# A recurrence and a two-layer FFN on one core: every two-operand elementwise operation but the masked decays goes to VectorE

## The chip, the cores and the metric

The kernel runs on one core of one Trainium2 chip, as one launch. The core has TensorE (PE in the rows; PEld is its weight load), VectorE (DVE), ScalarE (ACT), GpSimd (POOL) and SyncE (SP), which here only issues the loads and stores. The metric is the device time of one execution in microseconds, lower is better.

## The reference

The first half is a chunked linear recurrence over 4 x 8 heads, 768 tokens, head size 32, state size 16; the second half is an FFN on the recurrence's output.

```
for c in range(nc):                       # chunks of 32 tokens
    L = np.exp(cum[:, :, :, None] - cum[:, :, None, :]) * causal
    M = np.einsum('bhin,bhjn->bhij', Cc, Bc) * L
    y_intra = np.einsum('bhij,bhjd->bhid', M, xc)
    y_inter = np.einsum('bhin,bhnd->bhid', Cc, state) * np.exp(cum)[:, :, :, None]
    y[:, :, sl] = y_intra + y_inter
    state = decay_full * state + sum_j(Bc x xc * decay_from_j)
...
x = attn_out.transpose(0, 2, 1, 3).reshape(B * S, H * D)      # 3072 x 256
h = x @ w_in                                                  # 256 x 2048
g = np.maximum(h, 0.0) + np.log1p(np.exp(-np.abs(h)))         # softplus
return (g @ w_out).astype(np.float32)                         # 2048 x 256
```

`w_in` and `w_out` arrive as 64-bit floats and are turned into 32-bit floats on the chip.

## The kernel before

**Units.** The recurrence is worked in 24 units of 128 tokens (4 batches of 6), named by a number i: `un4` is the loaded data of unit 4. For each unit the kernel makes the masked decays `rm` (`decays`, L292, on GpSimd), the scores `sp` (TensorE), their product `m` (`weigh`, L350, VectorE, reads PSUM), the scaled B `bp` (`scale_b`, L307), the scaled C in a spread layout `r_apart` (`scale_c`, L320, two halves of 64 rows), the new state (`update`, L375) from `zp` (L364), the spread state `tb` (`spread`, L383), and the output `yp` (L393 and L407). `y` (`grow`, L417) is the scaled output; ScalarE rounds it to `xh` (L419) and the low part `xl` is what is left (`rest`, L424). From unit 8 on, B and C are laid out on the chip by `split_unit` (L198 on ScalarE, L199 on VectorE: `c_all`, `b_rows`).

**FFN.** Tokens go in 6 groups j of 512 (four units), features in 16 slices k of 128. `first` (L503) makes `hp` of (j, k) from three products: high weights by `xh`, high by `xl`, low by `xh`. ScalarE applies softplus (`e`, L523) and rounds it (`gh`, L530), VectorE takes the low part `gl` (L531), and `second` (L543) adds three products into the two accumulators `acc` of group j. `hp0_14` in a row of the order is group 0, slice 14; the profile's rows leave the numbers out.

**Weights.** 16 steps, each 512 columns; even steps are `w_in`, odd ones `w_out`, and step w opens slices k = w and w + 1 (for even w). A step is: ScalarE rescales (L475), VectorE does three bit operations (L477, L479, L481), ScalarE casts the high part `wih` or `woh` (L484), and the low part `wil` or `wol` is subtracted (L486). The tile `w` has two buffers.

**Who does what.** Five kinds of work (`bp`, `r_apart`, `tb`, `xl`, `wil`/`wol`) go to VectorE for the numbers in a table and to GpSimd for the rest:

```
V_BP = (0, 2, 7)
V_CC = (0, 1, 2, 6, 7)
V_TB = (2, 3, 4, 6)
V_XL = (2, 4, 7)
WL_V = (2, 7, 10, 11, 15)
```

**Order.** Up to unit 3 an order written out by hand (`ORDER`) is kept on every engine; its instructions appear under the line of a helper, L119. From there a scheduler orders the instructions of each engine from its own estimates of their lengths. Each engine then runs its instructions strictly in that order, and one that waits holds up all behind it. SyncE's order of loads is the same before and after the change.

Of the kernel before, what the change touches and what calls it, by code (L numbers as in the profile page):

```python
# [10 lines left out]
F32 = mybir.dt.float32  # L11
# [4 lines left out]
ALU = mybir.AluOpType  # L16
PSUM = bass.MemoryType.PSUM

P = 128
# [39 lines left out]
LAG = 8  # L59
LATE = (1, 1, 1, 1, -1, -2, -1, -1)  # L60
V_LAG = (0, 0, 1, 0, 0, 2, 0, 0)

V_BP = (0, 2, 7)
V_CC = (0, 1, 2, 6, 7)
V_TB = (2, 3, 4, 6)
V_XL = (2, 4, 7)
WL_V = (2, 7, 10, 11, 15)


def constants():  # L70
# [26 lines left out]
def recurrence_then_ffn(ctx: ExitStack, tc: tile.TileContext, fst, un, at, al, w_in, w_out, const, outT):  # L97
# [24 lines left out]
    V, A, Pl, PE = (InOrder(e) for e in (nc.vector, nc.scalar, nc.gpsimd, nc.tensor))  # L122
# [153 lines left out]
    def x_parts(t0):  # L276
        j = max(i for i in range(len(sizes)) if starts[i] <= t0)
        if j not in xparts:
            xparts[j] = [p3.tile([P, 2, 512], F32R, tag=f"x{v}", name=f"x{v}_{j}", bufs=2) for v in "hl"]
        return xparts[j], t0 - starts[j]  # L280
# [4 lines left out]
    mid = defaultdict(dict)  # L285
# [17 lines left out]
    def scale_b(i):  # L303
        b, u = divmod(i, NU)
        if u < NU - 1:
            bp = mid[i]["bp"] = p2.tile([P, NH, N], F32, tag="bp", name=f"bp{i}")
            (V if i in V_BP else Pl).tensor_tensor(  # L307
                bp,
                un_s[i][:, U_B:U_C].rearrange("p (h n) -> p h n", n=N),
                f_tok[b][0][:, u, :].unsqueeze(2).broadcast_to([P, NH, N]),  # L310
                op=ALU.mult,
            )

    def scale_c(i):
        b, u = divmod(i, NU)
        if u > 0:
            cc = mid[i]["cc"] = r_apart[i % 2]
            for g in range(2):
                rows = slice(64 * g, 64 * g + 64)
                (V if i in V_CC else Pl).tensor_tensor(  # L320
                    cc[rows, g],
                    un_s[i][rows, U_C:U_S].rearrange("p (c i) -> p c i", i=SUB),
                    f_row[b][rows, u, :NC].unsqueeze(2).broadcast_to([64, NC, SUB]),
                    op=ALU.mult,
                )
# [53 lines left out]
    def spread(i):  # L379

        if i % NU > 0:
            tb = mid[i]["tb"] = p2.tile([P, 2, 2, D], F32, tag="tb", name=f"tb{i}")
            (V if i in V_TB else Pl).tensor_tensor(  # L383
                tb,
                state[i - 1].rearrange("p (e d) -> p e d", d=D).unsqueeze(1).broadcast_to([P, 2, 2, D]),
                bd.rearrange("p (q e) -> p q e", e=2).unsqueeze(3).broadcast_to([P, 2, 2, D]),
                op=ALU.mult,
            )
# [32 lines left out]
    def rest(i):  # L421
        (xh, xl), c0 = x_parts(i * P)
        hi = xh[:, :, c0 : c0 + P].bitcast(F32)
        (V if i in V_XL else Pl).tensor_tensor(xl[:, :, c0 : c0 + P], mid.pop(i)["y"], hi, op=ALU.subtract)  # L424

    def attend_scores(i):
        decays(i)
        for g in range(2):
            score(i, g)
            weigh(i, g)  # L430
        scale_b(i)
        scale_c(i)

    def attend_values(i):
        for f in (spread, update, read, within, grow, rest):
            f(i)
# [24 lines left out]
    def split_stages(step):  # L461
        raw = raws.pop(step)
        q = step // 2
        if step % 2 == 0:
            fs = slice(q * 256, q * 256 + 256)
            cut = "p (c f) -> p c f", {"c": 2}
            hi, lo = wih[:, :, fs], wil[:, :, fs]
        else:
            ks = slice(2 * q, 2 * q + 2)
            cut = "p (k e) -> p k e", {"k": 2}  # L470
            hi, lo = woh[:, ks, :], wol[:, ks, :]
        low, high = raw[:, :, 0], raw[:, :, 1]
        w = p2.tile([P, 512], I32, tag="w", name=f"w{step}")
        wf = w.bitcast(F32)
        A.activation(wf, high.bitcast(F32), AF.Copy, scale=REBIAS)  # L475
        yield
        V.tensor_scalar(w, w, 3, None, op0=ALU.logical_shift_left)  # L477
        yield
        V.scalar_tensor_tensor(w, high, SIGN, w, op0=ALU.bitwise_and, op1=ALU.bitwise_or)  # L479
        yield  # L480
        V.scalar_tensor_tensor(w, low, 29, w, op0=ALU.logical_shift_right, op1=ALU.bitwise_or)  # L481
        yield
        r = wf.rearrange(cut[0], **cut[1])
        A.copy(hi, r)  # L484
        yield
        (V if step in WL_V else Pl).tensor_tensor(lo, r, hi.bitcast(F32), op=ALU.subtract)  # L486

    def split_w(step):
        for _ in split_stages(step):
            pass  # L490
# [89 lines left out]
    def step_w(i):  # L580
        if i not in stages:
            stages[i] = split_stages(i)
        next(stages[i], None)

    def both(f, i):
# [19 lines left out]
        "W": step_w,  # L605
        "D": decays,
        "B": scale_b,
        "C": scale_c,
        "S": lambda i: both(score, i),
        "M": lambda i: both(weigh, i),  # L610
        "U": update,
        "T": spread,
        "H": first_half,
        "R": read,
        "I": within,
        "G": grow,
        "X": rest,
        "zero": lambda _: Pl.memset(c_rows.bitcast(F32), 0.0),
    }
# [92 lines left out]
```

## Time and profile before

| | |
|---|---|
| median of 3 runs | 355.83 us (354.56 to 356.6) |
| the profiled execution | 354.56 us |
| its span, first to last instruction | 352.6 us |
| TensorE busy | 332.8 us, 94% |
| VectorE busy | 196.0 us, 56% |
| ScalarE busy | 168.4 us, 48% |
| GpSimd busy | 114.0 us, 32% |
| mean granted TensorE clock | 0.98 |

The busy shares are means over stages that differ, so a stage has to be looked at by itself. TensorE's matmuls are pipelined: one of 512 columns is listed with about 0.39 us while the next begins 0.23 us later. The time outside the span is 1.96 us.

### The profile page before, as it was taken

What the parts mean: (1) busy time and instruction counts of PE and PEld (TensorE: products, weight loads), DVE (VectorE), ACT (ScalarE), POOL (GpSimd) and SP (SyncE); (2) the same over time, 40 slices, a digit from 0 to 9 for tenths busy, and PEclk for the clock granted to TensorE, in tenths of its full rate; (3) what the DMA queues carried; (4) which work ended last, traced back from release to release, by engine and by line L of the source; (5) the groups of instructions that cost most, each with busy time, mean ns of one, the idle gap of its engine ahead of it and who ended that gap; (6) DMA issues with size and microseconds to landing.
All of it is one profiled execution on the core that took longest, in us unless ns stands there. A gap on an engine that the chain in (4) does not pass through costs nothing.

```text
span 352.6 us, 5070 instructions
## 1 busy us (share of the span) xinstructions
PE 332.8 (94%) x1882; PEld 252.0 (71%) x1882; DVE 196.0 (56%) x300; ACT 168.4 (48%) x297; POOL 114.0 (32%) x142
## 2 busy tenths in 40 slices
PE   6878985999999999999999999999999999999995
PEld 3533653567677877787877787787787788888884
DVE  1676999799984545553653553754363523132231
ACT  2311835584665535454644544645353534344450
POOL 6576943557631125323143322323512000000000
PEclk9689999899999999999999999999999999999999
DMA  7889745364210752141543222552303100001001
GB/s 203 222 196 335 252 136 187 120 257 144 51 70 8 214 152 91 30 135 48 162 121 109 65 82 71 140 161 93 91 30 89 31 2 0 0 23 40 0 2 59
DMA packets 22264, 37.23 MB, mean 106 GB/s; under 512 B 1632, under 2 KB 12896, under 8 KB 22240
## 3 DMA queue, kind: packets, MB, share of 16 engines
q1 hardware_dynamic: 22240, 36.91, 34.6%
q8 instruction: 15, 0.25, 0.3%
q14 instruction: 9, 0.07, 0.1%
HBM read 29.46 MB, written 3.24 MB: 93 GB/s over the span
## 4 chain that ended last, share of the span: by engine, by line
PE 76%; DMA 9%; DVE 8%; issue 2%; SPq 2%; ACT 1%; DVEq 0%; ACTq 0%
PE acc L543 33%; PE hp L503 32%; DMA wraw<-in_w_out 3%; DMA gg<-gd 3%; PE yp L407 3%; DVE w L479 2%; PE yp L393 2%; PE sp L339 2%; SPq L128 2%; DMA head_c<-in_fst 2%; DVE gl L531 1%; DMA c_rows<-c_all 1%; DVE w L477 1%; DVE w L481 1%; PE zp L364 1%
## 5 line engine op out<-in xcount | busy, mean ns | idle before, releaser
L531 DVE TENSOR_TENSOR gl<-e,gh 128x512 fp32r<-128x512 f32 x96 | 71.5, 746 | 83.0 <-ACT gh L530 82.3
L530 ACT CAST gh<-e 128x512 fp32r<-128x512 f32 x96 | 59.3, 620 | 65.2 <-PE acc L543 64.2
L503 PE MATMUL hp<-xh,wih 128*128 128x512 f32 (+1 forms) x192 | 77.2, 405 | 6.3 <-ACT wih L484 5.1
L523 ACT ACTIVATE e<-hp 128x512 f32<-128x512 f32 x96 | 56.6, 595 | 49.6 <-DVE gl L531 42.3
L543 PE MATMUL acc<-gl,woh 128*128 128x512 f32 x192 | 75.0, 390 | 0.0
L503 PE MATMUL hp<-xl,wih 128*128 128x512 f32 (+1 forms) x192 | 74.9, 391 | 0.0
L543 PE MATMUL acc<-gh,wol 128*128 128x512 f32 x192 | 74.9, 393 | 0.0
L503 PE MATMUL hp<-xh,wil 128*128 128x512 f32 (+1 forms) x192 | 74.3, 390 | 0.0
L543 PE MATMUL acc<-gh,woh 128*128 128x512 f32 x192 | 73.1, 392 | 0.2 <-DVE o L552 0.2
L503 PEld LDWEIGHTS hp<-xh,wih 128*128 128x128 f32 x192 | 36.1, 188 | 19.4 <-ACT wih L484 6.0
L292 POOL TENSOR_SCALAR_AFFINE_SELECT rm<-fc 128x1024 f32<-128x1024 f32 x20 | 32.1, 1605 | 47.8 <-DVE m L350 47.7
L543 PEld LDWEIGHTS acc<-gh,woh 128*128 128x128 f32 x192 | 36.0, 188 | 8.2 <-issue 0.8
L503 PEld LDWEIGHTS hp<-xh,wil 128*128 128x128 f32 x192 | 36.1, 188 | 8.0 <-issue 0.2
L543 PEld LDWEIGHTS acc<-gh,wol 128*128 128x128 f32 x192 | 36.0, 188 | 7.9 <-issue 0.2
L543 PEld LDWEIGHTS acc<-gl,woh 128*128 128x128 f32 x192 | 36.1, 188 | 7.5
L503 PEld LDWEIGHTS hp<-xl,wih 128*128 128x128 f32 x192 | 36.4, 189 | 6.5 <-issue 0.2
L350 DVE TENSOR_TENSOR m<-sp,rm 128x512 f32<-128x512 f32 x40 | 26.2, 684 | 14.0 <-PE sp L339 12.5
L199 DVE SCALAR_TENSOR_TENSOR c_all<-un,kb,c_all 128x512 fp32r<-128x512 f32 x16 | 17.3, 1084 | 10.4 <-ACT c_all L198 10.2
L424 POOL TENSOR_TENSOR xl<-y,xh 128x256 fp32r<-128x256 f32 x18 | 14.0, 780 | 25.8 <-ACT xh L419 25.2
L320 POOL TENSOR_TENSOR r_apart<-un,fr 64x128 f32<-64x128 f32 x32 | 17.1, 534 | 14.1 <-DMA un<-in_un 10.1
L307 POOL TENSOR_TENSOR bp<-un,ft 128x128 f32<-128x128 f32 x15 | 7.4, 491 | 42.1 <-DMA un<-in_un 23.7
L383 POOL TENSOR_TENSOR tb<-state,kb 128x128 f32<-128x128 f32 x16 | 11.9, 744 | 23.6 <-DVE state L375 23.0
(96 smaller groups left out, 306.5 us busy)
## 6 DMA issues: line engine op xcount, KB each, us to landing
un<-in_un SPq DMA_DIRECT2D x16, 768.0 KB, 4.5
wraw<-in_w_in SPq DMA_DIRECT2D x8, 512.0 KB, 7.8
wraw<-in_w_out SPq DMA_DIRECT2D x8, 512.0 KB
c_rows<-c_all SPq DMA_DIRECT2D x32, 128.0 KB, 2.4
gg<-gd SPq DMA_DIRECT2D x16, 192.0 KB
out_t<-o SPq DMA_DIRECT2D x12, 256.0 KB
un<-in_fst SPq DMA_DIRECT2D x4, 576.0 KB, 9.6
head_c<-in_fst SPq DMA_DIRECT2D x8, 128.0 KB, 6.5
```

Of the source, the lines that this page charges most:

```text
L199: V.scalar_tensor_tensor(out, raw, g, out.bitcast(F32), op0=ALU.mult, op1=ALU.add)
L292: Pl.affine_select(out=rm.rearrange("p h c i -> p (h c) i"), in_=fc[:, u].rearrange("p h c -> p (h c)").unsqueeze(2).broadcast_to([P, NH * ...
L320: (V if i in V_CC else Pl).tensor_tensor(cc[rows, g], un_s[i][rows, U_C:U_S].rearrange("p (c i) -> p c i", i=SUB), f_row[b][rows, u, :NC]. ...
L350: V.tensor_tensor(mid[i]["m"][:, 4 * g : 4 * g + 4].rearrange("p h t -> p (h t)"), mid[i].pop(("sp", g)), mid[i]["rm"][:, 4 * g : 4 * g + ...
L383: (V if i in V_TB else Pl).tensor_tensor(tb, state[i - 1].rearrange("p (e d) -> p e d", d=D).unsqueeze(1).broadcast_to([P, 2, 2, D]), bd.r ...
L407: PE.matmul(yp[32 * hh : 32 * hh + 32, g * P : (g + 1) * P], un_s[i][:, U_X + h * D : U_X + (h + 1) * D], m[:, h, :], start=u == 0, stop=u ...
L424: (V if i in V_XL else Pl).tensor_tensor(xl[:, :, c0 : c0 + P], mid.pop(i)["y"], hi, op=ALU.subtract)
L503: PE.matmul(h[:, c0:c1], w[:, c, fs], x[:, c, c0:c1], start=i == 0, stop=i == 5)
L523: A.activation(e, h, AF.Softplus)
L530: A.copy(gh, e)
L531: V.tensor_tensor(gl, e, gh.bitcast(F32), op=ALU.subtract)
L543: PE.matmul(acc[e][:, :n], w[:, k, es], g, start=k == 0 and i == 0, stop=k == NFT - 1 and i == 2)
```

## The change

The five tables go away, and each operation that chose an engine from one is VectorE's always. Nothing else is edited.

```diff
--- before.py
+++ after.py
@@ -59,12 +59,6 @@
 LAG = 8
 LATE = (1, 1, 1, 1, -1, -2, -1, -1)
 V_LAG = (0, 0, 1, 0, 0, 2, 0, 0)
-
-V_BP = (0, 2, 7)
-V_CC = (0, 1, 2, 6, 7)
-V_TB = (2, 3, 4, 6)
-V_XL = (2, 4, 7)
-WL_V = (2, 7, 10, 11, 15)
 
 
 def constants():
@@ -304,7 +298,7 @@
         b, u = divmod(i, NU)
         if u < NU - 1:
             bp = mid[i]["bp"] = p2.tile([P, NH, N], F32, tag="bp", name=f"bp{i}")
-            (V if i in V_BP else Pl).tensor_tensor(
+            V.tensor_tensor(
                 bp,
                 un_s[i][:, U_B:U_C].rearrange("p (h n) -> p h n", n=N),
                 f_tok[b][0][:, u, :].unsqueeze(2).broadcast_to([P, NH, N]),
@@ -317,7 +311,7 @@
             cc = mid[i]["cc"] = r_apart[i % 2]
             for g in range(2):
                 rows = slice(64 * g, 64 * g + 64)
-                (V if i in V_CC else Pl).tensor_tensor(
+                V.tensor_tensor(
                     cc[rows, g],
                     un_s[i][rows, U_C:U_S].rearrange("p (c i) -> p c i", i=SUB),
                     f_row[b][rows, u, :NC].unsqueeze(2).broadcast_to([64, NC, SUB]),
@@ -380,7 +374,7 @@
 
         if i % NU > 0:
             tb = mid[i]["tb"] = p2.tile([P, 2, 2, D], F32, tag="tb", name=f"tb{i}")
-            (V if i in V_TB else Pl).tensor_tensor(
+            V.tensor_tensor(
                 tb,
                 state[i - 1].rearrange("p (e d) -> p e d", d=D).unsqueeze(1).broadcast_to([P, 2, 2, D]),
                 bd.rearrange("p (q e) -> p q e", e=2).unsqueeze(3).broadcast_to([P, 2, 2, D]),
@@ -421,7 +415,7 @@
     def rest(i):
         (xh, xl), c0 = x_parts(i * P)
         hi = xh[:, :, c0 : c0 + P].bitcast(F32)
-        (V if i in V_XL else Pl).tensor_tensor(xl[:, :, c0 : c0 + P], mid.pop(i)["y"], hi, op=ALU.subtract)
+        V.tensor_tensor(xl[:, :, c0 : c0 + P], mid.pop(i)["y"], hi, op=ALU.subtract)
 
     def attend_scores(i):
         decays(i)
@@ -483,7 +477,7 @@
         r = wf.rearrange(cut[0], **cut[1])
         A.copy(hi, r)
         yield
-        (V if step in WL_V else Pl).tensor_tensor(lo, r, hi.bitcast(F32), op=ALU.subtract)
+        V.tensor_tensor(lo, r, hi.bitcast(F32), op=ALU.subtract)
 
     def split_w(step):
         for _ in split_stages(step):
```

100 operations move (17 `bp`, 34 `r_apart`, 17 `tb`, 21 `xl`, 11 low parts of weights). GpSimd keeps `rm` and the memsets. The scheduler makes a new order from this. In after.py all lines behind the tables are six numbers lower, so that the helper's L119 is L113 there and w's L477 is L471.

VectorE around the start of weight step 1, behind the hand-written part, before (`r_apart0` is `r_apart` of the even units):

```order
L119 TENSOR_TENSOR m3_336<-sp3_1_311,rm3_263 128x512
L119 SCALAR_TENSOR_TENSOR w2_224<-wraw2_167,w2_224 128x512
L383 TENSOR_TENSOR tb4_427<-state3_289,kb_77 128x128
L477 TENSOR_SCALAR w1_393<-w1_393 128x512
L119 TENSOR_TENSOR y3_351<-yp3_329,gg3_228 128x256
L479 SCALAR_TENSOR_TENSOR w1_393<-wraw1_261,w1_393 128x512
L119 TENSOR_TENSOR wil_86<-w2_224,wih_85 128x2x256
L119 TENSOR_TENSOR y2_359<-yp2_315,gg0_203 128x256
L481 SCALAR_TENSOR_TENSOR w1_393<-wraw1_261,w1_393 128x512
```

and after:

```order
L113 TENSOR_TENSOR m3_336<-sp3_1_311,rm3_263 128x512
L377 TENSOR_TENSOR tb4_427<-state3_289,kb_77 128x128
L113 SCALAR_TENSOR_TENSOR w2_224<-wraw2_167,w2_224 128x512
L301 TENSOR_TENSOR bp4_423<-un4_273,ft0_155 128x128
L314 TENSOR_TENSOR r_apart0_82<-un4_273,fr0_186 64x128 x2
L471 TENSOR_SCALAR w1_393<-w1_393 128x512
L113 TENSOR_TENSOR y3_351<-yp3_329,gg3_228 128x256
L113 TENSOR_TENSOR wil_86<-w2_224,wih_85 128x2x256
L113 TENSOR_TENSOR xl_0_304<-y0_301,xh_0_303 128x2x128
L473 SCALAR_TENSOR_TENSOR w1_393<-wraw1_261,w1_393 128x512
```

`bp4` and `r_apart0`, which read the load `un4`, now stand ahead of w1's first step; the low parts `wil` and `xl` stand between the steps.

VectorE around the last bit operation of weight step 14, before:

```order
L481 SCALAR_TENSOR_TENSOR w9_687<-wraw9_579,w9_687 128x512
L477 TENSOR_SCALAR w14_737<-w14_737 128x512
L531 TENSOR_TENSOR gl0_9_667<-e0_9_664,gh0_9_666 128x512
L479 SCALAR_TENSOR_TENSOR w14_737<-wraw14_603,w14_737 128x512
L199 SCALAR_TENSOR_TENSOR c_all8_902<-un8_735,kb_77,c_all8_902 128x512
L199 SCALAR_TENSOR_TENSOR b_rows8_901<-un8_735,kb_77,b_rows8_901 128x512
L481 SCALAR_TENSOR_TENSOR w14_737<-wraw14_603,w14_737 128x512
L350 TENSOR_TENSOR m7_819<-sp7_0_817,rm7_815 128x512
L350 TENSOR_TENSOR m7_819<-sp7_1_821,rm7_815 128x512
L199 SCALAR_TENSOR_TENSOR c_all9_1009<-un9_877,kb_77,c_all9_1009 128x512
L199 SCALAR_TENSOR_TENSOR b_rows9_1008<-un9_877,kb_77,b_rows9_1008 128x512
L477 TENSOR_SCALAR w11_763<-w11_763 128x512
```

and after, the part that ends with the same operation:

```order
L525 TENSOR_TENSOR gl0_9_667<-e0_9_664,gh0_9_666 128x512
L471 TENSOR_SCALAR w14_737<-w14_737 128x512
L480 TENSOR_TENSOR wol_88<-w9_687,woh_87 128x512
L525 TENSOR_TENSOR gl0_10_706<-e0_10_703,gh0_10_705 128x512
L193 SCALAR_TENSOR_TENSOR c_all9_1009<-un9_877,kb_77,c_all9_1009 128x512
L473 SCALAR_TENSOR_TENSOR w14_737<-wraw14_603,w14_737 128x512
L344 TENSOR_TENSOR m7_819<-sp7_0_817,rm7_815 128x512
L193 SCALAR_TENSOR_TENSOR b_rows9_1008<-un9_877,kb_77,b_rows9_1008 128x512
L525 TENSOR_TENSOR gl0_11_754<-e0_11_751,gh0_11_753 128x512
L344 TENSOR_TENSOR m7_819<-sp7_1_821,rm7_815 128x512
L471 TENSOR_SCALAR w11_763<-w11_763 128x512
L475 SCALAR_TENSOR_TENSOR w14_737<-wraw14_603,w14_737 128x512
```

`gl0_10`, `gl0_11`, both halves of `m7`, `c_all9`, `b_rows9` and the first step of w11 stood behind w14's last step (L481, now L475) and now stand ahead of it.

TensorE in front of `hp0_14`, before:

```order
L543 MATMUL acc1_0_641<-gl0_7_615,woh_87 128x512
L543 MATMUL acc1_0_641<-gh0_7_614,wol_88 128x512
L543 MATMUL acc0_0_640<-gh0_8_636,woh_87 128x512
L543 MATMUL acc0_0_640<-gl0_8_637,woh_87 128x512
L543 MATMUL acc0_0_640<-gh0_8_636,wol_88 128x512
L543 MATMUL acc1_0_641<-gh0_8_636,woh_87 128x512
L543 MATMUL acc1_0_641<-gl0_8_637,woh_87 128x512
L407 MATMUL yp7_837<-m7_819,un7_594 32x128 x8
L503 MATMUL hp0_14_858<-xh_0_303,wih_85 128x512
```

and after:

```order
L537 MATMUL acc1_0_641<-gl0_8_637,woh_87 128x512
L537 MATMUL acc1_0_641<-gh0_8_636,wol_88 128x512
L537 MATMUL acc0_0_640<-gh0_9_666,woh_87 128x512
L537 MATMUL acc0_0_640<-gl0_9_667,woh_87 128x512
L537 MATMUL acc0_0_640<-gh0_9_666,wol_88 128x512
L537 MATMUL acc1_0_641<-gh0_9_666,woh_87 128x512
L537 MATMUL acc1_0_641<-gl0_9_667,woh_87 128x512
L537 MATMUL acc1_0_641<-gh0_9_666,wol_88 128x512
L401 MATMUL yp7_837<-m7_819,un7_594 32x128 x8
L497 MATMUL hp0_14_858<-xh_0_303,wih_85 128x512
```

All six products of slice 9 and the last one of slice 8, which stood behind `hp0_14`, are now ahead of it.

## Rows read from the trace of the kernel before

**Rows 1.** Windows: length, busy PE, PEld, DVE, ACT, POOL, then PEclk, DMA, GB/s.

```profile
36.00:113.00 77.00, 70.73 (x405) 50.07 (x406) 68.32 (x100) 46.99 (x83) 41.52 (x41) 0.98 0.41 136
113.00:340.00 227.00, 226.80 (x1270) 180.79 (x1269) 104.21 (x156) 109.23 (x190) 50.45 (x67) 1.00 0.26 77
```

**Rows 2.** TensorE's timeline: start, us, instruction, [idle before, releaser].

```profile
53.38 0.50 PE L503 MATMUL hp<-xh,wih 128*128 128x512 f32 x1 [1.39 <-ACT wih L484]
...
61.31 0.50 PE L503 MATMUL hp<-xh,wih 128*128 128x512 f32 x1 [3.74 <-ACT wih L484]
...
83.74 0.50 PE L503 MATMUL hp<-xh,wih 128*128 128x512 f32 x1
```

**Rows 3.** A window behind the long stop: TensorE busy, granted clock, DMA.

```profile
62.00:65.00 3.00, 3.00 (x8) 0.50 0.78 268
```

**Rows 4.** ScalarE's timeline in front of `hp0_14`.

```profile
81.31 0.62 ACT L484 CAST wih<-w 128x512 fp32r<-128x512 f32 x1 [0.68 <-DVE w L481]
```

**Rows 5.** VectorE's timeline, and one decay on GpSimd.

```profile
32.89 0.43 DVE L477 TENSOR_SCALAR w<-w 128x512 int32<-128x512 int32 x1 [2.47 <-ACT w L475]
...
49.55 1.67 POOL L292 TENSOR_SCALAR_AFFINE_SELECT rm<-fc 128x1024 f32<-128x1024 f32 x1 [2.16 <-DVE m L350]
49.99 1.75 DVE L479 SCALAR_TENSOR_TENSOR w<-wraw,w 128x512 int32<-128x512 int32 x1
51.67 0.41 DVE L477 TENSOR_SCALAR w<-w 128x512 int32<-128x512 int32 x1
52.00 0.68 DVE L481 SCALAR_TENSOR_TENSOR w<-wraw,w 128x512 int32<-128x512 int32 x1
52.60 0.68 DVE L479 SCALAR_TENSOR_TENSOR w<-wraw,w 128x512 int32<-128x512 int32 x1
...
59.30 0.58 DVE L320 TENSOR_TENSOR r_apart<-un,fr 64x128 f32<-64x128 f32 x2
...
80.39 0.88 DVE L481 SCALAR_TENSOR_TENSOR w<-wraw,w 128x512 int32<-128x512 int32 x1
```

**Rows 6.** GpSimd's timeline: `bp4` waits for its load.

```profile
33.64 0.88 POOL L307 TENSOR_TENSOR bp<-un,ft 128x128 f32<-128x128 f32 x1 [3.35 <-DMA un<-in_fst]
```

**Rows 7.** VectorE's groups, 32.5 to 81.1 us: count, busy, mean ns, idle before.

```profile
L479 DVE SCALAR_TENSOR_TENSOR w<-wraw,w 128x512 int32<-128x512 int32 x11 | 9.8, 898 | 0.1
L481 DVE SCALAR_TENSOR_TENSOR w<-wraw,w 128x512 int32<-128x512 int32 x11 | 9.7, 886 | 0.1
L531 DVE TENSOR_TENSOR gl<-e,gh 128x512 fp32r<-128x512 f32 x10 | 9.6, 957 | 0.8 <-ACT gh L530 0.8
L477 DVE TENSOR_SCALAR w<-w 128x512 int32<-128x512 int32 x11 | 6.6, 609 | 3.2 <-ACT w L475 3.2
L350 DVE TENSOR_TENSOR m<-sp,rm 128x512 f32<-128x512 f32 x6 | 4.1, 681 | 1.3 <-PE sp L334 1.3
L199 DVE SCALAR_TENSOR_TENSOR b_rows<-un,kb,b_rows 128x512 fp32r<-128x512 f32 x1 | 1.8, 1769 | 0.0
...
L119 DVE TENSOR_TENSOR xl<-y,xh 128x256 fp32r<-128x256 f32 x1 | 0.8, 830 | 0.0
...
L424 DVE TENSOR_TENSOR xl<-y,xh 128x256 fp32r<-128x256 f32 x1 | 0.4, 411 | 0.0
```

**Rows 8.** VectorE's groups, 290 to 340 us.

```profile
L531 DVE TENSOR_TENSOR gl<-e,gh 128x512 fp32r<-128x512 f32 x19 | 13.2, 693 | 36.7 <-ACT gh L530 36.7
```

**Rows 9.** VectorE's timeline: one `b_rows` that nothing slows.

```profile
196.69 0.74 DVE L199 SCALAR_TENSOR_TENSOR b_rows<-un,kb,b_rows 128x512 fp32r<-128x512 f32 x1
```

**Rows 10.** GpSimd's groups, 32.5 to 81.1 us.

```profile
L486 POOL TENSOR_TENSOR wil<-w,wih 128x512 fp32r<-128x512 f32 x4 | 6.6, 1644 | 8.3 <-ACT wih L484 8.2
L486 POOL TENSOR_TENSOR wol<-w,woh 128x512 fp32r<-128x512 f32 x4 | 5.9, 1468 | 1.4 <-ACT woh L484 1.3
L292 POOL TENSOR_SCALAR_AFFINE_SELECT rm<-fc 128x1024 f32<-128x1024 f32 x3 | 4.8, 1602 | 4.3 <-DVE m L350 4.3
```

**Rows 11.** The chain that ended last: start, us, what.

```profile
109.39 1.36 PE acc L543 x6
```

## Prediction

> **What bounds the kernel now.** I read the stages first, then TensorE's waits in the stage that has any, then VectorE's queue in front of them.
>
> The windows [rows 1] show two stages behind the start. From 113 us on, TensorE is busy 226.80 of 227.00 us and VectorE 104.2: nothing that VectorE or GpSimd does there ends a wait, and both have room. From 36 to 113 us VectorE is busy 68.3 of 77 us and TensorE 70.7. So the change is decided between 33 and 113 us, where the weights are split, units 4 to 9 of the recurrence run, and VectorE is nearly full.
>
> In that stage TensorE's timeline [rows 2] shows two long stops, 1.39 us before `hp0_6` at 53.38 and 3.74 us before `hp0_8` at 61.31. Both wait for ScalarE's cast of a split of w_in, which itself waits for VectorE's last `w` step. After the second stop the granted clock is 0.50 (1.2 GHz) from 62 to 65 us [rows 3], at 1.00 before; three microseconds at half speed lose 1.5. The third row is `hp0_14` at 83.74, which starts with no wait: its weights were cast from 81.31 to 81.93 [rows 4], 1.8 us ahead. That is the last weight pair, so the last gate of this kind.
>
> **What the change moves.** 100 operations leave GpSimd, which keeps the masked decays (`rm`). The order rows show the rest: the program order of VectorE changes as well. I follow VectorE's queue from the first step of w1 (`L477`, 32.89 [rows 5]) to the last step of w14 (`L481`, starts 80.39, 0.88 long with its overlap, so about 81.2), because that step opens `hp0_14`.
>
> *Start.* `bp4` and both `r_apart` of unit 4 now stand ahead of w1 on VectorE. GpSimd had to wait for unit 4's load until 33.64 [rows 6]. VectorE will wait there instead, then run three operations of 0.29 each (two `r_apart` take 0.58 [rows 5]): 33.64 + 0.87 = 34.5, so w1 starts 1.6 us later, and behind it `y3`, `y2` and their casts, which open the rest of `hp0_0`. TensorE's stops at 53 and 61 us can take in that delay.
>
> *Added.* Between the two steps after.py has 20 more operations that were GpSimd's: 8 low parts of weights, 4 of x, 4 `r_apart`, 2 `bp`, 2 `tb`. Successive operations of 512 columns start 0.60 apart though each lasts 0.68 (52.00 and 52.60 [rows 5]), so an operation costs some 0.08 less than its duration: 8 x 0.60 + 4 x 0.33 (a 256-column `xl` lasts 0.41 [rows 7]) + 8 x 0.29 = 8.4 us.
>
> *Pulled ahead.* Seven operations that stood behind w14's last step now stand in front of it: `gl0_10`, `gl0_11`, both `m7`, `c_all9`, `b_rows9`, the first step of w11. 4 x 0.60 + 2 x 0.66 (0.74 alone [rows 9], less 0.08) + 0.33 = 4.1 us.
>
> *Removed.* In this window VectorE's operations with both inputs in SBUF last longer than alone. The groups of the window [rows 7] against the unhindered durations (0.68 and 0.41 for the `w` steps [rows 5], 693 ns for `gl` late in the program [rows 8], 0.74 for `b_rows` [rows 9], 411 for `xl`): 11 x (898 - 680) + 11 x (886 - 680) + 10 x (957 - 693) + 11 x (609 - 410) + 1.03 + 0.42 = 10.9 us. Operations that read PSUM show nothing (`m` 681). Three decays run in the window [rows 10], and one costs 1.07 (a `w` step of 1.75 that starts under a decay at 49.55, instead of 0.68 [rows 5]). The decays stay, three of them again, so 3.2 us stay, and 7.7 us go.
>
> *Waits of VectorE itself.* In the window they are 0.8 (`gl`), 1.3 (`m`) and 3.2 - 2.47 = 0.7 (`w`) [rows 5, 7], together 2.8. A later queue absorbs between none and all; I take half, 1.4.
>
> The queue: +1.6 + 8.4 + 4.1 - 7.7 - 1.4 = **+5.0 us** at w14, between +3.6 (all absorbed) and +6.4 (none). What VectorE gives up to contention and what it takes over nearly cancel; the late start and the seven operations make the difference.
>
> **What TensorE feels.** w14's last step then ends at 81.2 + 5.0 = 86.2 and the cast 0.73 later, 86.9. On TensorE the new order puts seven `acc` products ahead of `hp0_14` that stood behind it, 7 x 0.23 = 1.6 us (six take 1.36 us in the chain [rows 11]): without any gate it would get there at 83.74 + 1.6 = 85.3. So it waits 1.6 us; between 0.2 (85.5) and 3.0 (88.3).
>
> Two small waits follow. In after.py the low part `wil` of w14 ends eight operations behind w14's last step (three of 512 columns, five small: 3 x 0.60 + 5 x 0.29 = 3.2 us at most); GpSimd had done it beside. TensorE has the cast's 0.73 and some 1.8 us of other products until it needs it, so it waits 0.7 at most, and I take 0.3. `xl` of unit 7, which opens the rest of `hp1_0`, comes eight operations later (four of 512 columns, three of 256 or alike, one small, 3.7 us) with a decay's 1.07 in between, while TensorE has some 4.5 us of its own: again 0.3. From there both orders fall together, at the products of `acc` with k = 15, and the last 240 us are TensorE's own.
>
> Sum: 1.6 + 0.3 + 0.3 = +2.2 us on the profiled execution's 354.56, 356.8. The median of the runs shown is 355.83, 1.27 above it; I forecast medians, so **358.0**, with its own range from 356.0 (a gate of 0.2, no small waits) to 359.4 (3.0 and 0.6). A change of 0.5%, 1.8 us, is about what a measurement of this kernel can tell from none; the forecast stands just over it.
>
> **Weighed against a page.** The rows above say that GpSimd's help is worth 8.4 us of VectorE's queue and costs 7.7 in stalls, so taking it back is about even. The Trainium skill, Perfetto Trace Analysis, "Optimizing Scalar/DVE Operations", says that offloading from a saturated VectorE may make sense, but that the two share a read port, so that it might not help. By its first half alone taking the work back costs the whole 8.4; the trace agrees with its second.
>
> **Rivals.**
>
> *The wait for ScalarE moves into VectorE's queue (slower).* GpSimd stood 8.2 and 1.3 us waiting for ScalarE's casts before its 8 low parts of weights [rows 10]; that cost nothing there. On VectorE everything behind stands too. For it: VectorE has no room. Against it: the new order leaves two to four operations between a `w` step and its low part. If half of the 9.5 us shows, the gate opens 4.75 later: 358.0 + 4.75 = 362.7; all of it, 367.5. It decides from about 2 us on, since TensorE has no slack left at `hp0_14`.
>
> *Freed of GpSimd, VectorE opens the early gates sooner (faster).* GpSimd's low parts were busy 6.6 + 5.9 = 12.5 us in the window [rows 10]. If each blocked VectorE for as long as it ran, 12.5 instead of 7.7 us go, the queue at w14 is even (+0.2), `hp0_14` is not gated, and the stops at 53 and 61 us shrink with the slow clock after them. Those are 1.39 + 3.74 + 1.5 = 6.6 us; half gone is 355.83 - 3.3 = 352.5. Against it: the late start of 1.6 us comes before both gates, and the measured stalls are 10.9, decays included. The Trainium skill, SBUF — State Buffer, "Who interferes with whom", has this as its rule: the shared port pair is an exclusive lock and the loser blocks fully. Under the decay at 49.55 the trace agrees (1.07 us lost, until the decay's end).
>
> *Hidden anyway.* VectorE's later queue stays under TensorE's 85.3 and nothing shows: 355.8, just under the forecast's own range, and counted with it.
>
> **How the numbers follow.** Forecast 0.50 (of it 0.26 within 0.5% of the median, up to 357.6, and 0.24 above), the wait for ScalarE 0.28, the faster gates 0.22 (0.18 of it over 0.5% faster). Faster 0.18, same 0.26 + 0.04 = 0.30, slower 0.24 + 0.28 = 0.52. The range goes from the faster rival, 352.5, to a little over the half price of the slower one, 363.5.
>
> **What would show it.** Right: VectorE's `gl` and `w` steps at 0.68 except under a decay, where one loses about a microsecond; GpSimd busy only with decays; w1's first step near 34.5; the cast for `hp0_14` near 86 with a wait of 1 to 3 us before it; no difference after some 114 us. Wrong: waits of VectorE for ScalarE's `wih` and `woh` casts that sum to several microseconds (first rival); a shorter stop at 61 us with the clock held at 1.00 (second); or any new TensorE wait after 114 us, which no row of before announces.

## The result, and the profile after

| | before | after |
|---|---|---|
| median, 20 runs each | 355.44 us (354.09 to 357.21) | 357.34 us (355.92 to 361.7) |
| ratio, 95% interval | | 1.005, 1.0032 to 1.0068 |
| the profiled execution / its span | 354.56 / 352.6 us | 357.09 / 355.4 us |
| group 0's accumulators done (first `o<-acc`) | 112.83 us | 114.97 us |
| from there to the end of the span | 239.8 us | 240.4 us |

The changed kernel is 0.5% slower. Its run of 361.7 us counts as a slow one and is left out of the ratio. The profiled executions stand 2.5 us apart, the medians 1.9. Of the 2.8 us between the spans, 2.14 have come about by the time group 0's accumulators are done, so the place to look is where the prediction looked, ahead of 113 us.

The windows of the changed kernel (length, busy PE, PEld, DVE, ACT, POOL, then PEclk, DMA, GB/s) answer to [rows 1] and [rows 3]:

```profile
36.00:113.00 77.00, 73.72 (x411) 51.98 (x412) 69.77 (x135) 45.93 (x83) 10.79 (x6) 0.96 0.40 134
113.00:340.00 227.00, 226.80 (x1267) 180.18 (x1266) 118.82 (x210) 108.93 (x189) 19.10 (x12) 1.00 0.26 77
62.00:65.00 3.00, 3.00 (x13) 1.67 (x12) 2.88 (x7) 2.78 (x6) 0.00 (x0) 1.00 0.79 296
```

From 113 us on TensorE is as busy as before, although VectorE has 14.6 us more to do. From 36 to 113 TensorE is busier than before, and the slow clock at 62 to 65 us is gone. Read alone, these rows look like an improvement. Its timeline shows where the time went (start, us, instruction, [idle before, releaser]; these four answer to [rows 2] and [rows 4]):

```profile
36.00 0.58 PE L113 MATMUL hp<-xl,wih 128*128 128x256 f32 x1 [5.90 <-DVE xl L113]
...
85.05 0.43 PE L401 MATMUL yp<-m,un 128*32 128x128 f32 x8 [1.42 <-DVE m L344]
86.63 0.50 PE L497 MATMUL hp<-xh,wih 128*128 128x512 f32 x1 [1.16 <-ACT wih L478]
...
89.88 0.78 PE L497 MATMUL hp<-xh,wil 128*128 128x512 f32 x1 [0.32 <-DVE wil L480]
```

The stops of 1.39 and 3.74 us at 53 and 61 us are gone. In their place stands one of 5.90 us that ends at 36.00, just outside the window that I had chosen, and the forecast stop around `hp0_14` (1.42 and 1.16 us). A table of idle and clock by stretch makes it an account. First the kernel before, then the changed one, same columns:

```profile
28.00:36.00 8.00, 5.61 (x55) 3.37 (x55) 5.53 (x10) 1.98 (x4) 4.53 (x5) 1.00 1.05 353
36.00:40.00 4.00, 4.00 (x35) 3.05 (x36) 3.96 (x7) 3.62 (x6) 3.38 (x4) 1.00 0.60 231
52.00:66.00 14.00, 8.87 (x29) 5.39 (x30) 11.72 (x20) 8.71 (x16) 6.18 (x4) 0.88 0.57 193
84.00:93.00 9.00, 7.86 (x42) 6.03 (x42) 9.00 (x16) 4.75 (x10) 4.49 (x6) 1.00 0.41 119
```

```profile
28.00:36.00 8.00, 1.71 (x21) 0.60 (x19) 4.64 (x13) 1.57 (x3) 1.81 (x1) 0.78 1.05 358
36.00:40.00 4.00, 4.00 (x15) 2.92 (x15) 2.89 (x7) 1.72 (x3) 0.00 (x0) 0.59 0.51 194
52.00:66.00 14.00, 14.00 (x73) 10.12 (x73) 11.89 (x26) 7.07 (x14) 1.95 (x1) 1.00 0.45 153
84.00:93.00 9.00, 6.47 (x43) 4.65 (x43) 8.96 (x19) 3.93 (x8) 2.26 (x2) 0.81 0.39 118
```

Loss is idle time plus length times what is missing of the clock (in 28 to 36 us idle time alone, since the clock falls there while TensorE stands: it is 1.00 from 28 to 32 us and 0.50 from 33 us on). Before: 2.39 + 0 + (5.13 + 1.68) + 1.14 = 10.3 us. After: 6.29 + 1.64 + 0 + (2.53 + 1.71) = 12.2, and 0.39 and 0.37 of idle at 40 to 52 and 66 to 84 us make 12.9. That is 2.6 us more, against the 2.14 measured; the rest, I take it, lies ahead of 28 us or in the means of the clock. So the change traded 6.8 us of stops around 60 us for 5.5 more around 36 and 3.1 more around 87.

VectorE's timeline shows what the stop at 36 us waits for:

```profile
33.43 0.29 DVE L301 TENSOR_TENSOR bp<-un,ft 128x128 f32<-128x128 f32 x1 [3.32 <-DMA un<-in_fst]
33.64 0.58 DVE L314 TENSOR_TENSOR r_apart<-un,fr 64x128 f32<-64x128 f32 x2
34.25 0.43 DVE L471 TENSOR_SCALAR w<-w 128x512 int32<-128x512 int32 x1
34.59 0.42 DVE L113 TENSOR_TENSOR y<-yp,gg 128x256 f32<-128x256 f32 x1
34.92 0.68 DVE L113 TENSOR_TENSOR wil<-w,wih 128x512 fp32r<-128x512 f32 x1
35.52 0.42 DVE L113 TENSOR_TENSOR xl<-y,xh 128x256 fp32r<-128x256 f32 x1
```

The last row is the low part of x of unit 0, which GpSimd had finished at 27.34, in the row below of the kernel before. Here it stands behind `bp4`, which waits 3.32 us for unit 4's load, and ends at 35.94.

```profile
26.61 0.73 POOL L119 TENSOR_TENSOR xl<-y,xh 128x256 fp32r<-128x256 f32 x1
```

The experiments ask which part of the change costs what: that place, the wait for the load, the gate at `hp0_14`, or the later units.

### The profile page after: what moved, and what is told of

Same layout as the page of the kernel before. It is cut to its first block, busy times and chain, and to the rows that moved or that the text cites. A ratio compares the mean times of both kernels' runs of the same rounds, so it can differ in the third digit from the quotient of the medians.

```text
span 355.4 us, 4966 instructions
## 1 busy us (share of the span) xinstructions
PE 334.6 (94%) x1882; PEld 252.5 (71%) x1882; DVE 214.8 (60%) x400; ACT 168.1 (47%) x297; POOL 45.5 (13%) x42
## 4 chain that ended last, share of the span: by engine, by line
PE 77%; DMA 12%; DVE 6%; ACT 1%; SPq 1%; issue 1%; ACTq 0%
PE hp L497 34%; PE acc L537 33%; DMA un<-in_fst 5%; PE yp L401 3%; PE yp L387 2%; PE sp L333 2%; DMA un<-in_un 2%; DMA head_c<-in_fst 2%; DMA wraw<-in_w_in 2%; SPq L122 1%; DMA c_rows<-c_all 1%; PE zp L358 1%; DVE gl L525 1%; DVE w L473 1%; DVE w L475 1%
## 5 line engine op out<-in xcount | busy, mean ns | idle before, releaser
L525 DVE TENSOR_TENSOR gl<-e,gh 128x512 fp32r<-128x512 f32 x96 | 67.1, 699 | 67.5 <-ACT gh L524 67.2
L537 PE MATMUL acc<-gh,woh 128*128 128x512 f32 x192 | 74.2, 396 | 0.2 <-DVE o L546 0.2
L286 POOL TENSOR_SCALAR_AFFINE_SELECT rm<-fc 128x1024 f32<-128x1024 f32 x20 | 33.3, 1666 | 207.2 <-DVE m L344 203.1
L192 ACT ACTIVATE c_all<-un,kb 128x512 fp32r<-128x512 f32 x16 | 11.6, 723 | 14.5 <-DMA un<-in_un 14.5
L193 DVE SCALAR_TENSOR_TENSOR c_all<-un,kb,c_all 128x512 fp32r<-128x512 f32 x16 | 15.2, 952 | 3.9 <-ACT c_all L192 3.8
L193 DVE SCALAR_TENSOR_TENSOR b_rows<-un,kb,b_rows 128x512 fp32r<-128x512 f32 x16 | 16.9, 1059 | 0.1
L469 ACT ACTIVATE w<-wraw 128x512 f32<-128x512 f32 x14 | 9.5, 676 | 14.9 <-DMA wraw<-in_w_out 7.3
L401 PE MATMUL yp<-m,un 128*32 128x128 f32 x320 | 14.3, 280 | 1.8 <-DVE m L344 1.8
## 6 DMA issues: line engine op xcount, KB each, us to landing
un<-in_fst SPq DMA_DIRECT2D x4, 576.0 KB, 12.2
```

Source lines behind the costliest of these rows:

```text
L192: A.activation(out, raw, AF.Copy, scale=be)
L193: V.scalar_tensor_tensor(out, raw, g, out.bitcast(F32), op0=ALU.mult, op1=ALU.add)
L286: Pl.affine_select(out=rm.rearrange("p h c i -> p (h c) i"), in_=fc[:, u].rearrange("p h c -> p (h c)").unsqueeze(2).broadcast_to([P, NH * ...
L401: PE.matmul(yp[32 * hh : 32 * hh + 32, g * P : (g + 1) * P], un_s[i][:, U_X + h * D : U_X + (h + 1) * D], m[:, h, :], start=u == 0, stop=u ...
L525: V.tensor_tensor(gl, e, gh.bitcast(F32), op=ALU.subtract)
L537: PE.matmul(acc[e][:, :n], w[:, k, es], g, start=k == 0 and i == 0, stop=k == NFT - 1 and i == 2)
```

## The experiments

Every edit also gives the scheduler other work, so that each kernel has an order of its own; a difference is that of edit and new order together. Medians are of 12 runs, but of 5 for units_only, 6 for loads_only and 7 for low_parts_only. Ratios are to the kernel before (median 355.4 to 355.7 us in each set).

**By stage and by kind.** Four kernels take a part of the change alone.

```diff
 late_only: units from 10 on; weights by the old table
-(V if i in V_BP else Pl)              # the same for V_CC, V_TB, V_XL
+(V if i in V_BP or i >= 10 else Pl)
 early_only: units below 10, and all low parts of weights
+(V if i in V_BP or i < 10 else Pl)
 low_parts_only: the low parts of weights alone
-(V if step in WL_V else Pl).tensor_tensor(lo, ...)
+V.tensor_tensor(lo, ...)
 units_only: bp, r_apart, tb and xl of all units; weights by the old table
-(V if i in V_BP else Pl)              # the same for V_CC, V_TB, V_XL
+V
```

> Units 10 to 23 of the recurrence have their four small operations on VectorE as in the changed kernel; units 0 to 9 and all weights follow the tables of before. The gate theory (VectorE's queue reaches weight step 14 and m of unit 7 some 4.7 us later, and TensorE stops there) and the head-of-line theory (VectorE waits for the loads of units 4, 5 and 7 with everything behind it) both act before 113 us: the time stays that of before, 355.4, within 0.6. A theory of VectorE's load over the whole span expects about half of the loss, 356.2 to 356.8, with new TensorE waits after 114 us.

> The complement: units 0 to 9 and all low parts of weights on VectorE, units 10 to 23 by the tables of before. Gate and head-of-line theory: the time of the changed kernel, 357.3, within 0.8, with stops of 1 to 3 us in front of hp0_14. Load over the whole span: about half of the loss, 356.2 to 356.8.

> Only the low parts of the weights move to VectorE; the recurrence's small operations keep the tables of before. Gate theory: 6.6 us of low parts (11 at 0.60) are added to VectorE and the stalls from GpSimd's long low parts go, so the queue at weight step 14 moves by less than 2 us and the time lies between 354.5 and 357. Head-of-line theory: no operation that waits for a load has moved, so nothing is lost and the stops at 53 and 61 us shrink: 351 to 355.5.

> Only the recurrence's small operations (bp, r_apart, tb, xl) move to VectorE; the low parts of the weights keep the table of before. Head-of-line theory: VectorE waits for the loads of units 4, 5 and 7 as in the changed kernel, so the whole loss is here: 357 to 360, with the long TensorE stop near 30 to 36 us. Gate theory: some 4 us of small operations are added while GpSimd's low parts keep stalling VectorE by 1 us each, so the queue at weight step 14 is 4 to 6 us late: 356.5 to 360 too; the two are told apart by whether the stop near 36 us or the one in front of hp0_14 carries it.

| | median | ratio, interval |
|---|---|---|
| late_only | 356.08 us | 1.0016, 0.9998 to 1.0033 |
| early_only | 356.72 us | 1.0037, 1.0006 to 1.0067 |
| low_parts_only | 353.46 us | 0.9931, 0.9901 to 0.9960 |
| units_only | 362.27 us | 1.0187, 1.0161 to 1.0213 |

The early units carry most of the loss. The times alone do not settle it: early_only's 356.72 lies in both forecasts set down for it, and late_only's 356.08 just outside of both. The later units alone make no difference that can be told from none, though from group 0's accumulators to the end their traces need 240.4 us in late_only and units_only, and 239.8 in early_only and low_parts_only as before. (It stays so in all runs below: 240.4 or 240.5 wherever `bp` and `r_apart` of the last units are VectorE's, 239.7 or 239.8 where they are not. So that is what 0.6 of the 2.8 us hang on.) Of the other two, low_parts_only lies where the head-of-line theory alone had it, and units_only is slower than either theory allowed (360 at most). The parts don't add up: 2.2 us gained by the weights' low parts and 6.6 lost by the recurrence's operations make +4.4, where the whole change has +1.9. The kernel units_only has the stop of the changed kernel, shorter and later, `hp<-xl,wih` at 38.31 after 5.04 us for `xl`, so that stop alone does not explain its 6.6. The kernel low_parts_only has none there, but the old one before `hp0_8`, 3.01 us at 62.73.

**Three repairs of the changed kernel.** One moves unit 0's low part of x ahead in the hand-written order, one opens the weights of `hp0_14` earlier, one gives `bp4` and `r_apart` of unit 4 back to GpSimd.

```diff
 x0_early: ORDER
-... W0 X1 zero M3 w6 W2 I3 W2 G3 W2 X0 w4 X3 ...
+... W0 X1 X0 zero M3 w6 W2 I3 W2 G3 W2 w4 X3 ...
 w14_early: W_ORDER
-(0, 1, 4, 3, 2, 6, 10, 8, 5, 7, 12, 9, 14, 11, 13, 15)
+(0, 1, 4, 3, 2, 6, 10, 8, 5, 7, 12, 14, 9, 11, 13, 15)
 unit4_back: bp and r_apart
-V.tensor_tensor(
+(Pl if i == 4 else V).tensor_tensor(
```

> The changed kernel with one word of the hand-written order moved: the low part of x of unit 0 stands right behind that of unit 1 instead of at the end, so on VectorE it is ahead of bp and r_apart of unit 4, which wait for that unit's load. Head-of-line theory: the 5.9 us stop of TensorE near 30 to 36 us and the half-speed clock behind it go, and the time falls by 1 to 3 us to 354.5 to 356.5. Gate theory: VectorE's queue is unchanged in length, weight step 14 still ends near 85 to 86, and the time stays within 0.8 us of 357.3.

> The changed kernel with weight step 14 loaded and split before step 9. Gate theory: w14's last bit operation ends 2 to 3 us earlier, the wait for its cast in front of hp0_14 (1.16 us) goes, the one for m of unit 7 (1.42 us) may stay or shrink; the time falls by 1 to 2.5 us to 355 to 356.5, unless w9 becomes the next late one. Head-of-line theory: nothing before hp0_14 changes, the time stays within 0.6 of 357.3.

> The changed kernel with only bp and r_apart of unit 4 (three operations) back on GpSimd. Head-of-line theory: VectorE no longer stands 3.3 us for the load of unit 4, the TensorE stop near 36 us shrinks below 3 us, and the time falls by 1 to 3 us. Gate theory: the queue at weight step 14 comes 1.4 us earlier at most (the late start), so 0.5 to 1.4 us of the 1.9 come back: 356 to 356.9.

| | median | ratio, interval |
|---|---|---|
| x0_early | 355.42 us | 0.9992, 0.9964 to 1.0020 |
| w14_early | 356.55 us | 1.0034, 1.0008 to 1.0059 |
| unit4_back | 354.65 us | 0.9966, 0.9944 to 0.9988 |

Against the changed kernel's 357.34, putting one operation of 0.42 us elsewhere gives 1.9 us back, and three small operations that wait for a load 2.7. The gate gives 0.8, and its interval overlaps that of the changed kernel, though its trace has no stop for `wih` at `hp0_14` any more: that gate looks like the smaller part. Its 356.55 lies between the forecasts of the two theories, and its early stop is even longer (6.31 us), so the gate's share is not settled by it. TensorE's timeline of x0_early shows what comes after the repair:

```profile
33.34 1.13 PE L328 MATMUL sp<-un 64*128 64x512 f32 x4 [0.98 <-DMA un<-in_fst]
...
36.83 1.22 PE L387 MATMUL yp<-r_apart,tb 128*128 128x256 f32 x2 [1.55 <-DVE y L113]
...
61.61 0.50 PE L497 MATMUL hp<-xh,wih 128*128 128x512 f32 x1 [2.84 <-ACT wih L478]
```

The 5.90 us shrink to 0.98 and 1.55 and one of 0.48 between them, and the stop before `hp0_8` is back. The slow clock, which I had expected to go with the long stop, did not go: it is 0.50 from 36 to 40 us, 0.90 from 40 to 52 and 0.89 from 52 to 66, together 4.7 us lost, where the changed kernel has 1.6. So a stop 5.90 us long gives back only 1.9. In unit4_back VectorE does not wait for unit 4's load; `xl` still stands behind a wait of 1.48 us for a ScalarE rescale, and the stop for it is 2.89 us instead of 5.90.

**Which operations of the recurrence, and whether the repairs add.** My theory after those runs was that the wait for unit 4's load costs, and that `xl` is only what stands behind it.

```diff
 loads_only: from before, bp and r_apart to V; the rest by the old tables
 low_xl: from before, low parts of weights and xl to V; bp, r_apart, tb by the old tables
 no_loads: low_xl, and tb to V
 both_back: from after, the edits of x0_early and unit4_back
```

> This kernel takes the kernel before and gives VectorE only the operations that read a unit's load, the scaled B and both halves of the scaled C of every unit; the low parts of the weights and of x and the spread state keep their old tables. Theory (what costs in the change are the operations that wait for a load in front of VectorE's queue): TensorE stops near 36 us by 3 us or more, VectorE shows a wait of 2 us or more for unit 4's load, and the time is 1.0 to 1.8% above before (359 to 362). Rival (the cost is the plain length of the moved recurrence operations on a full engine): the scaled B and C are only some 10 of the 23 moved operations before 113 us and carry less than half of the 6.7 us that all recurrence operations alone had cost, so 0.3 to 0.8% above before (356.5 to 358.4).

> This kernel gives VectorE the low parts of the weights and of x alone; scaled B, scaled C and spread state keep their old tables. Theory (waits for loads cost): as with the spread state, 0.990 to 0.996. Rival (the place of the x low parts in VectorE's queue is what starves TensorE, since its stop at 36 us names the low part of x): a stop at 36 us of 3 us or more without any VectorE wait for a load, ratio above 1.000.

> This kernel gives VectorE every low part, of the weights and of x, and every spread state; the scaled B and C, which read a load, keep their old tables, so that GpSimd waits for the load of unit 4. Theory (waits for loads cost): no TensorE stop of more than 2 us before 40 us and the time stays within 0.3% of the kernel that moves the weights' low parts alone, 0.9931, so ratio 0.990 to 0.996. Rival (the length of the operations costs): the x low parts and spread states take back more than half of that gain, ratio 0.998 to 1.006.

> This kernel is the changed one with both repairs: the scaled B and C of unit 4 go back to GpSimd and the low part of x of unit 0 moves right behind that of unit 1 in the hand-written order. If the two repairs take away one and the same wait, as the theory of the wait for unit 4's load has it, the time is that of the better one, 0.9966 of before, between 0.994 and 0.999. If they mend two different things, the gains add, 1.9 and 2.7 us from 357.3, so 352.8 or 0.992, with no TensorE stop over 1.5 us between 28 and 60 us.

| | median | ratio, interval |
|---|---|---|
| loads_only | 360.27 us | 1.0144, 1.0101 to 1.0187 |
| low_xl | 356.78 us | 1.0027, 1.0000 to 1.0054 |
| no_loads | 357.06 us | 1.0023, 0.9999 to 1.0046 |
| both_back | 355.21 us | 0.9991, 0.9968 to 1.0015 |

The theory fell by low_xl. It moves no operation that reads a load, and still it loses the 0.7% that the weights' low parts had gained. The spread state adds nothing to that (no_loads). Two timelines of low_xl, VectorE and then TensorE:

```profile
32.20 0.43 DVE L477 TENSOR_SCALAR w<-w 128x512 int32<-128x512 int32 x1 [1.89 <-ACT w L475]
...
33.48 0.89 DVE L119 TENSOR_TENSOR wil<-w,wih 128x512 fp32r<-128x512 f32 x1
34.29 1.16 DVE L119 TENSOR_TENSOR xl<-y,xh 128x256 fp32r<-128x256 f32 x2
```

```profile
34.96 0.38 PE L119 MATMUL hp<-xl,wih 128*128 128x256 f32 x1 [4.14 <-DVE xl L119]
```

Here VectorE waits for a ScalarE rescale (1.89 us), not for a load, and unit 0's `xl` stands behind that just the same. So what makes this stop is the place in the queue, behind whatever waits there.

loads_only is as slow as the theory had it, but not in the place it named: VectorE waits 3.29 us for a ScalarE rescale ahead of `bp4` and not at `bp4` itself; its one wait for a load is 2.5 us at a later `bp`. TensorE stops for 2.71 us at 33.38, for the load itself, and for 3.23 at 64.23, and it runs at half speed behind both (windows, columns as above):

```profile
35.00:45.00 10.00, 9.09 (x47) 5.93 (x45) 9.46 (x17) 5.46 (x10) 4.48 (x4) 0.50 0.64 220
65.00:70.00 5.00, 5.00 (x12) 2.46 (x11) 3.07 (x5) 1.56 (x3) 2.54 (x2) 0.50 0.54 206
```

Busy 9.09 and 5.00 us at half the clock lose 4.5 and 2.5. That most of its loss is the clock's is worked out from these rows; no run takes the clock away.

The repairs do not add (both_back, 355.21 and not 352.8): its trace has the stop before `hp0_8` again, 2.59 us at 63.26, and a clock of 0.75 from 40 to 52 us, which loses 3.0. So part of what is won at 36 us is lost behind it. How much cannot be read from this profile, whose execution (356.49 us) is the slowest of the twelve.

**The place alone.** The last run puts unit 0's `xl` ahead in low_xl; nothing else is edited. The scheduler's order changes with that one word all the same: by the names in the traces VectorE's orders differ at 103 of 332 places, ScalarE's at 60 of 297 and TensorE's, from 40 us on, at 242 of 1882.

```diff
 low_xl_x0: ORDER
-... W0 X1 zero M3 w6 W2 I3 W2 G3 W2 X0 w4 X3 ...
+... W0 X1 X0 zero M3 w6 W2 I3 W2 G3 W2 w4 X3 ...
```

> This kernel gives VectorE the low parts of the weights and of x, as an earlier one, and moves the low part of x of unit 0 right behind that of unit 1 in the hand-written order; scaled B, scaled C and spread state keep their old tables. Theory (what the x low parts cost is the place of unit 0's on VectorE, behind the operations of weight steps 2 and 1, which stopped TensorE for 4.4 us near 35 us): that stop shrinks below 1.5 us and the time comes back to that of the kernel that moves the weights' low parts alone, ratio 0.989 to 0.996. Rival (the cost is their length on a full VectorE, or every early stop only comes back at a later gate): the stop near 35 us goes, another of 2 us or more appears between 50 and 80 us, and the ratio stays at 0.998 to 1.006.

It measured 353.11 us, ratio 0.9928, interval 0.9902 to 0.9953; the pair's ratios differ by 0.0099 or 3.5 us. Its timelines, VectorE and TensorE:

```profile
30.90 0.75 DVE L119 TENSOR_TENSOR xl<-y,xh 128x256 fp32r<-128x256 f32 x2
```

```profile
33.60 0.28 PE L119 MATMUL hp<-xl,wih 128*128 128x256 f32 x1
...
63.67 0.50 PE L503 MATMUL hp<-xh,wih 128*128 128x512 f32 x1 [2.46 <-ACT wih L484]
```

Both low parts of x now come in one piece ahead of w2's last step and all of w1's, and the product that reads them starts without a wait, so the stop of 4.14 us is gone by the place alone. The 3.5 us are those of the place and of the new order behind it; no run parts the two. Against the rival that I had set beside it, the gain stays although the stop before `hp0_8` returns. So the low parts, of weights and of x, cost nothing that can be told from none on VectorE in this order, and this kernel and low_parts_only, 0.7% faster than before, beat both kernels. Their profiled executions (354.03 and 354.49 us) lie 0.9 and 1.0 us above their medians, and TensorE's wait for `head_c` ends 1.8 and 2.8 us later in them than before (25.96 and 26.96 instead of 24.20), so I do not read from them where the 0.7% comes from.

## Why the prediction was right, and which step was not

**The stage.** Right. TensorE's rows after 113 us did not change, and late_only shows no loss that can be told from none. "No difference after some 114 us" was a little off: 0.6 us are lost there in the profiled execution, with the late `bp` and `r_apart`.

**VectorE's queue.** Right in the sum, +4.65 us where +5.0 was forecast, but in part by luck, since the terms miss in opposite directions: w14's last step starts at 85.24 and ends at 85.92 (81.27 before). Its terms:

- *Start* +1.6: w1's first step is at 34.25, +1.36. The wait for the load stands at `bp4`, as said.
- *Added and pulled ahead*: from the one step to the other, both counted, there are 93 operations instead of 66, the 20 + 7 more that were counted.
- *Removed* -7.7: VectorE's groups from 32.5 to 85.9 us answer to [rows 7].

```profile
L473 DVE SCALAR_TENSOR_TENSOR w<-wraw,w 128x512 int32<-128x512 int32 x11 | 8.4, 769 | 0.1
L525 DVE TENSOR_TENSOR gl<-e,gh 128x512 fp32r<-128x512 f32 x12 | 8.2, 682 | 0.0
L475 DVE SCALAR_TENSOR_TENSOR w<-wraw,w 128x512 int32<-128x512 int32 x11 | 7.4, 682 | 0.0
...
L301 DVE TENSOR_TENSOR bp<-un,ft 128x128 f32<-128x128 f32 x4 | 2.2, 540 | 5.7 <-DMA un<-in_fst 5.3 <-DMA un<-in_un 0.5
```

  `gl` and one `w` step run at 0.68 as forecast. What stays is 11 x (769 - 680) + 4 x (540 - 285) = 2.0 us, under decays, so that 8.9 us went rather than 7.7. Three decays were over by then, and two of them held up one operation each, by about the 1.07 that I had taken (a `bp` of 1.28 us at 44.43, a `w` step of 1.62 at 69.92). Under the third, at 54.61, VectorE was soon waiting for a load and lost nothing. The Trainium skill, SBUF — State Buffer, "Who interferes with whom", calls the shared ports an exclusive lock; a `bp` of 1.16 us at 86.03 instead of 0.29, beside a decay from 85.12 to 87.07, agrees. A `w` step at 85.24, beside the same decay, kept its 0.68; the rows do not say why.
- *VectorE's own waits* -1.4: this term had the wrong sign. They are some 3.5 us (without the 3.32 of the start) instead of 2.8, all of them for loads: two `bp` wait 1.95 and 0.47, and an `r_apart` at 39.86 waits 1.11. I let a later queue absorb waits for ScalarE and TensorE, which it did (`gl` 0.0, [rows 7] 0.8), and forgot that the moved operations bring waits of their own.

With these values the terms give 1.36 + 8.4 + 4.1 - 8.9 + 0.7 = 5.7, and 4.65 were measured. The 1.0 us between them lies in the three middle terms: from w1's first step to w14's last VectorE is busy 47.87 us instead of 45.26, 2.6 more, where they give 3.6.

**The gate.** Right. ScalarE's cast for `hp0_14` ends at 86.58, forecast 86.9; TensorE stops for 1.42 and 1.16 us in front of it (2.6 together; forecast 1.6, from 0.2 to 3.0) and 0.32 for `wil` (forecast 0.3). Without the two it would have come there at 84.05, not at the 85.3 of the forecast. The first of the two waits for `m7`, which stands just ahead of w14's last step. The wait for `xl` of unit 7 did not come. Not in the sum were the half-speed spell behind the gate (1.71 us in the window from 84 to 93) and the 1.14 us of idle that before has there.

**The step that failed** is the last clause of *Start*: "TensorE's stops at 53 and 61 us can take in that delay". They did take in a delay, but not one of 1.6 us. I followed `y3` and `y2` behind w1 and passed over `xl_0`, two rows behind `y3` in the same order listing, which GpSimd had had ready at 27.34 and which TensorE needed at 30.1. The stop of 5.90 us and the slow clock behind it cost 5.5 us more than before. The stops at 53 and 61 us with their slow clock, 6.8 us, went in return; what shows in the time is about the rest, the 3.1 us more around the gate and 0.8 of small stops. ScalarE's casts of w_in's steps (by the kernel's order of steps, those for slices 6, 10 and 8) show why the two stops went, before and then after:

```profile
52.71 0.62 ACT L484 CAST wih<-w 128x512 fp32r<-128x512 f32 x1 [4.12 <-DVE w L481]
...
54.25 0.61 ACT L484 CAST wih<-w 128x512 fp32r<-128x512 f32 x1
...
60.64 0.62 ACT L484 CAST wih<-w 128x512 fp32r<-128x512 f32 x1 [3.28 <-DVE w L481]
```

```profile
50.88 0.61 ACT L478 CAST wih<-w 128x512 fp32r<-128x512 f32 x1
...
60.11 1.23 ACT L478 CAST wih<-w 128x512 fp32r<-128x512 f32 x2 [4.19 <-DVE w L475]
```

The cast that opens `hp0_8` ends at 61.26 before and at 61.34 after. That gate did not move; TensorE came to it later, at 61.38, and so did not wait. The cast that opens `hp0_6` ends at 51.49 instead of 53.33, 1.8 us sooner in spite of the later start, but TensorE is not there until 55.50. That the whole came out at +1.9 against +2.2 is thus in part luck: the forecast had neither the 5.5 us around 36 us nor the 6.8 that went, and the two nearly cancel.

**The rivals.** Waits of VectorE for ScalarE's `wih` and `woh`: the list of its waits from 28 to 114 us has none,

```profile
DVE bp L301 <- DMA un<-in_fst: 5.3, 2, 3.3
DVE gl L525 <- ACT gh L524: 3.9, 2, 2.0
DVE r_apart L314 <- DMA un<-in_fst: 1.1, 1, 1.1
DVE bp L301 <- DMA un<-in_un: 0.5, 1, 0.5
```

(the two for `gl` end after 110 us) so the mechanism was right (a wait moves into VectorE's queue and holds all behind it) and the releaser wrong: loads, not casts. Earlier gates: the sign that I had named, no stop at 61 us and the clock at 1.00 behind it, did come, but not from an earlier gate at `hp0_8`. At `hp0_6` the gate did open 1.8 us earlier, as this rival has it, and the changed kernel could not use it, since TensorE was late from the stop at 36 us. That taking work from GpSimd can pay is shown by low_parts_only and low_xl_x0, 0.7% each. There the Trainium skill, Perfetto Trace Analysis, "Optimizing Scalar/DVE Operations", which warns that offloading between the two might not help, agrees with the runs as to the low parts: the nearly full VectorE took them back and the kernel became faster. The recurrence's operations, taken back alone (units_only), made it 1.9% slower.

**What stays open.** How much of each difference is the scheduler's new order; how the loss divides between unit 0's `xl` and the operations that wait for loads, since each repair alone brings all of the 1.9 us back and both together no more; why loads_only ran 10 us at half speed; what the 6.6 us of units_only are beyond its stop; and in which stretch the two best kernels gain.

## What to carry to other kernels

When work moves to an engine that runs in order, list each moved operation's reader and ask what now stands ahead of it: here moving one operation of 0.42 us, with the new order that the scheduler made of it, was worth 1.9 us in one kernel and 3.5 in another, while all low parts on VectorE, in the better order, cost nothing that shows. An operation that waits for a load belongs on an engine with nothing urgent behind it, however small it is. A repair at an early stop may be worth less than the stop (1.9 us for 5.90 here), so look up when the next gate opens, and what the clock does, before adding gains.

## What the runs showed of the hardware

The granted clock fell to 0.50 (1.2 GHz) in a stretch where TensorE then worked almost without a pause: busy 9.09 of 10 us in loads_only, behind a stop of 2.71. In the kernel before, 1.24 us of idle for the same load at 33.61 left the clock at 1.00. Shorter stops in a row went with it too: in x0_early it was 0.50 from 36 to 42 us, around stops of 0.98, 0.48 and 1.55 us, and in the changed kernel 0.50 from 88 to 89 us, behind 1.42 and 1.16. In low_xl_x0, on the other hand, the 2.46 us before `hp0_8` left it at 1.00 (63 to 66 us). The loads of the start also land at different times in the profiles, one execution of each kernel, though SyncE's order of loads is the same before and after: TensorE's wait for `head_c` ends at 24.20 before, 24.11 after and 26.96 in low_xl_x0.
